# A new order of all steps, with other buffers and other engines for some, in an attention and FFN kernel on one core

## The chip, the core and the metric

The kernel runs on one core of a Trainium2 chip. A core has TensorE (PE: matmuls, and the weight loads PEld beside them), VectorE (DVE), ScalarE (ACT), GpSimd (POOL) and SyncE (SP), whose queue starts the DMAs here. The time is that of one execution in device microseconds: a median of 245.04 us over 3 runs (244.92 to 245.08).

## The reference

Polysketch attention, whose result goes into a multiplicative FFN:

```python
# q, k, v: 4 x 4 x 1088 x 32;  S1, S2: 8 x 32
def phi(x):
    a = np.einsum('rd,bhsd->bhsr', S1, x)
    b = np.einsum('rd,bhsd->bhsr', S2, x)
    return np.einsum('bhsi,bhsj->bhsij', a, b).reshape(*x.shape[:-1], r * r)
q_p, k_p = (phi(q), phi(k))
kv = np.einsum('bhsf,bhsd->bhfd', k_p, v)
z = np.sum(k_p, axis=2)
num = np.einsum('bhsf,bhfd->bhsd', q_p, kv)
den = np.einsum('bhsf,bhf->bhs', q_p, z)[..., None] + 1e-06
x = (num / den), reordered to 4352 x 128
# w1, w2: 128 x 1024;  w3: 1024 x 1024;  w_out: 1024 x 128
a = x @ w1
b = x @ w2
h = a * b @ w3
out = h @ w_out
```

## The kernel before

The program is a list of 1179 small named steps, each of which issues one instruction or a few. Nothing is decided at run time: the table ORDER names every step in the order in which it is issued, and each engine, SP's DMA queue included, runs its own instructions in just that order (every instruction is chained to the one before it on its engine). A step that waits therefore holds up all later steps of its engine.

Four more tables go with ORDER. SLOTS says for each kind of buffer which slot every allocation takes, in order: `b` are the eight PSUM banks, `m`, `l`, `s`, `x`, `raw` and `q_m` SBUF slots. A slot that is taken again makes its new writer wait for the last reader of what it held. POOL is the set of steps that run on GpSimd, where such a step has a choice; CPV that of the PSUM copies that run on VectorE instead of ScalarE. WARM gives the numbers of idle matmuls in the steps warm0 to warm11, 27 at the start and 2, 3, 4, 4, 4, 1, 2, 1, 1, 2, 2 later.

The steps have names by stage:

- `s.` prepares the sketches S1 and S2.
- `k0.` to `k3.` are the batches of keys and values (`kr.` their rest rows): loads, a maximum, a split of k in a leading and a rest part, `gram` (many short matmuls, L659), the small chain `G`, `T`, `N` (L883 to L912) which gives the numbers by which queries are centred, `kp` (the features of k), `kv` (L769), and `kzt`, `kqt`.
- `q0.` to `q6.` are groups of queries (`qr.` the rest rows): transposes, the sketch products `A0`, `A1`, `C0`, `C1`, the chain of splits `sm`, `st`, `sh`, `sl` (L1137 to L1157 on VectorE), products `p01`, `p2`, `p12`, the denominator `dn`, `de`, `rc`, the features `phi`, their transposes `pt`, and the attention product `x`, with `xs`, `xt`, `xc`, `xT` for q0, whose last, `xT` (L1291), is what the first FFN matmul reads.
- `g0.` to `g7.` and `gr.` are the FFN on groups of 512 rows (`gr` 256): for each of eight chunks of the width, `a` and `b` (matmuls with w1 and w2, L1799 and L1809), `c` (a copy of a out of PSUM), `m` (the product, L1815) and `o` (the matmul with the folded w3 and w_out, L1835, and L1824 for `gr`).
- `w` steps split the FFN's weights, `f` steps fold w3 and w_out in one matrix.
- `h4.` and `h6.` do the groups 4, 5 and 6, 7 in pairs by a scheme of seven products: matmuls `a1` to `b7` (L1673), sums `m11` to `m22` and `T1` to `T4` on VectorE and GpSimd (L1685 to L1742), products `P1` to `P7` (L1759; two for low and high partitions run side by side), and the sums `k1` to `k9` that give the two outputs (L1767 to L1785).
- `oT`, `oS`, `st` transpose, scale and store an output (L1842, L1848, L1556; `st1` of the rest rows L1562).

Bulk loads have one more rule: each waits until the fourth bulk load ahead of it has landed.

Of the kernel before, what the change touches and what calls it, by code (L numbers as in the profile page):

```python
# [65 lines left out]
    g0.0c g0.1c h4.1ac h4.1ad h6.1bc h6.2ad k0.kT1 k1.kvc k2.kT1 k2.kq k3.kT0 k3.kT1 k3.kq q0.xc0  # L66
    q0.xc1 q6.xT0 q6.xT2
# [15 lines left out]
q0.al k0.Nf q0.phi0 q0.phi1 q0.A1 q0.smy w1.m1 k1.max q0.sty q0.shy k0.kv3 k0.kv1 k0.kv2 q0.sly s.KS k0.kvr kr1.tr
k0.kvm w1.m0 kr1.kT q0.p01 q1.C0 q1.C1 q0.C1 k0.kzt k2.loadr q0.pt0 q0.C1t q0.scy q0.p2 k0.kz q0.pt1 k0.kvc kr1.ab
k0.kqt q0.p12 q0.dn q0.de q0.rc w1.j0 q0.pc0 q0.pc1 q0.x0 k1.kT0 q0.x1 q0.xs0 q0.xs1 q0.xt0 w1.a0 q1.A0 k2.load
w0.load k1.lead0 q0.xc0 q0.xc1 k0.kq w1.a1 k2.max q0.xt1 k1.ab q0.xT0 q0.xT1 g0.4a q1.load g0.5a q1.sm w0.m1 q1.st
q1.Ct g0.4c g0.4b q1.sh q1.sl k1.rest0 g0.7b w0.c1 g0.7a k1.abt w0.j1 k1.gram0 w0.c0 s.RC q1.scy k1.gram1 kh2.load
q1.sca q2.tr g0.5c q1.al q1.p01 q1.p2 k1.gram2 k1.gram3 kr1.abc k1.gram4 w6.load w0.m0 g0.6b w0.j0 g0.7c g0.7m k1.Gm
q1.p12 k1.Gc g0.0a w2.load w0.a1 q1.dn q1.de q1.rc q1.bs k1.Gt g0.3a k1.Ga k1.T0 k2.kT1 k1.Gb g0.3c q1.restT g0.2a
q1.phi k1.T1 q1.pt0 g0.4m w0.a0 q2.max q2.l2 g0.6a k1.Ta k2.lead0 k2.rest0 g0.1a g0.2c k1.Tc g0.5b q3.tr g0.5m k1.Tb  # L90
q1.pc0 q1.pt1 g0.1b w9.load k1.N0 s.AR q2.l1 q2.rm v3.zero q1.pc1 k1.N1 q1.x g0.6c g0.1c k1.Na k1.Nr k3.zero k2.gram0
g0.1m k2.gram1 k2.gram2 q3.max k2.gram3 g0.0c k2.kT0 k1.Nb q1.xT k2.gram4 q3.l2 k2.ab q2.A0 q2.C0 q2.C1 q3.l1 k1.kp0
v1.zero w9.c k2.abt g1.5a g1.5c g1.1a q2.Ct g1.7a q2.At q3.rm q3.A0 k0.Nr q2.sm q3.C0 q3.C1 k2.Gm v1.loadr q2.st w2.m
q2.sh g1.1c g1.2a k1.kp1 g0.6m q3.Ct g1.0a g1.7b k3.load v1.load g1.5b q3.At k2.Gt k3.loadr w2.c k2.Ga g0.0b w9.j
q2.sl g1.7c w6.c g1.6a k1.kv0 q3.sm k2.Gb w5.load q2.sc q2.al g1.0c k2.Gc g1.7m q2.p01 q3.st k1.kv2 k1.kv3 q3.sh w9.m
k1.kv1 k2.T0 k1.kvr q3.sl q2.p2 k2.T1 q2.p12 q2.dn q2.de g1.4a q2.rc k3.max g0.3b g0.0m g1.1b kh3.load g1.4c k2.Ta
g1.2b q3.sc g1.2c w5.c k2.Tc k1.kvc k1.kqt k1.kq g0.3m q3.p01 g1.6c g1.3a g1.5m g1.3b q2.bs q2.phi0 q2.pT0 g1.2m g1.3c
# [1837 lines left out]
```

## Time and profile before

| | |
|---|---|
| time, median of 3 runs | 245.04 us |
| span of the profiled execution | 244.1 us |
| PE busy | 236.2 us (97%) |
| DVE busy | 206.7 us (85%) |
| POOL busy | 161.9 us (66%) |
| ACT busy | 123.5 us (51%) |
| moved by DMA | 22.06 MB |

The profiled execution's span is 0.9 us below the median: the span runs from its first instruction to its last. In rows of the timeline the columns are start, length, engine, line of the kernel, operation, output and inputs, tile shape and how often; what stands in brackets is the engine's idle time ahead of the row, with what ended it. In rows of the chain of waits that ended last there are only start, length and what ran.

### The profile page before, as it was taken

Reading aid. Unit: us, or ns where it says so; the run is one execution under the profiler, and the core shown is the slowest. Engines: PE = TensorE matmul, PEld = TensorE weight load, DVE = VectorE, ACT = ScalarE, POOL = GpSimd, SP = SyncE. Lnnn points to the kernel's source line nnn. Section 1 sums busy time; section 2 is a strip of 40 time slices with the busy share of each in tenths; the row PEclk is TensorE's granted clock in tenths of the full one; section 3 lists DMA queues with packets and bytes.
Section 4 is the critical chain, followed back from the end, with each engine's and each line's share of the span. In section 5 each row is a group of like instructions: output and inputs, shape, how many; then the busy total and the mean of one; then the engine's idle time right before and its main releaser. Section 6 shows DMA issues by size and latency. Waiting matters only on the chain.

```text
span 244.1 us, 6745 instructions
## 1 busy us (share of the span) xinstructions
PE 236.2 (97%) x2724; PEld 129.8 (53%) x2724; DVE 206.7 (85%) x421; ACT 123.5 (51%) x246; POOL 161.9 (66%) x203
## 2 busy tenths in 40 slices
PE   8998999899999999999999999999999999999994
PEld 5887454545545646766566444444443354463363
DVE  2876988999899998997899878498989789999792
ACT  3976957675666764593012914355651164730010
POOL 4576658344856998764583889929999425883670
PEclk9999999999999999999999999999999999999999
DMA  7959797078859897200000000360000000000054
GB/s 201 265 143 325 181 227 190 6 197 224 220 141 251 188 217 190 59 1 3 3 0 0 4 0 3 59 113 3 1 0 0 0 3 0 0 1 3 12 90 93
DMA packets 31935, 22.06 MB, mean 90 GB/s; under 512 B 21280, under 2 KB 26528, under 8 KB 31904
## 3 DMA queue, kind: packets, MB, share of 16 engines
q1 hardware_dynamic: 31360, 21.11, 35.1%
q8 instruction: 21, 0.34, 0.6%
q10 hardware_dynamic: 544, 0.52, 0.6%
q14 instruction: 10, 0.08, 0.1%
HBM read 19.40 MB, written 2.23 MB: 89 GB/s over the span
## 4 chain that ended last, share of the span: by engine, by line
PE 87%; DMA 5%; ACT 2%; POOL 2%; DVE 1%; issue 1%; POOLq 0%; SPq 0%
PE b_ps L1809 12%; PE ps_o L1835 12%; PE ps_X L1673 11%; PE a_ps L1799 11%; PE ps_o L1759 10%; PE ps_w3o L534 6%; PE ps_Y L1673 6%; PE ps_Z L1673 3%; PE ps_g L659 2%; PE ps_x L1527 2%; PE ps_ac L1374 2%; DMA qh<-in_q_dram 2%; DMA k<-in_k_dram 2%; PE ps_or L1824 2%; POOL ph L1208 1%; PE idle_ps L255 1%
## 5 line engine op out<-in xcount | busy, mean ns | idle before, releaser
L1673 PE MATMUL ps_X<-xd,wv 64*128 64x512 f32 x112 | 36.3, 593 | 0.0
L1799 PE MATMUL a_ps<-xT,w 128*128 128x512 f32 (+1 forms) x80 | 36.1, 562 | 0.0
L1809 PE MATMUL b_ps<-xT,w 128*128 128x512 f32 (+1 forms) x80 | 35.6, 555 | 0.0
L1804 ACT COPY ffa<-a_ps 128x512 f32<-128x512 f32 (+1 forms) x38 | 20.1, 540 | 29.2 <-PE a_ps L1799 26.7
L1707 POOL TENSOR_TENSOR hc<-hc 128x512 f32<-128x512 f32 x16 | 20.7, 1304 | 15.7 <-DVE hc L1685 15.5
L1835 PE MATMUL ps_o<-ab,w3o 128*128 128x512 f32 x64 | 29.6, 600 | 0.0
L1680 ACT COPY hc<-ps_X 128x512 f32<-128x512 f32 x38 | 21.3, 590 | 16.1 <-PE ps_X L1673 12.9
L1815 DVE TENSOR_TENSOR ab<-ffa,b_ps 128x512 f32<-128x512 f32 (+1 forms) x40 | 23.9, 623 | 4.9 <-PE b_ps L1809 4.1
L501 POOL TENSOR_TENSOR w3c<-w3c,cv_m 128x512 int32<-128x512 int32 x16 | 21.2, 1344 | 4.2 <-DVE w3c L495 4.1
L1673 PEld LDWEIGHTS ps_X<-xd,wv 64*128 64x128 f32 x112 | 14.9, 186 | 13.1 <-issue 10.9
L1799 PEld LDWEIGHTS a_ps<-xT,w 128*128 128x128 f32 x80 | 14.1, 189 | 13.9 <-issue 8.8
L1809 PEld LDWEIGHTS b_ps<-xT,w 128*128 128x128 f32 x80 | 14.4, 190 | 13.1 <-issue 8.1
L1673 PE MATMUL ps_Y<-xd,wv 64*128 64x512 f32 x48 | 19.7, 594 | 0.0
L1835 PEld LDWEIGHTS ps_o<-ab,w3o 128*128 128x128 f32 x64 | 11.6, 190 | 13.4 <-issue 13.0
L534 PEld LDWEIGHTS ps_w3o<-wo,w3T 128*128 128x128 f32 x128 | 15.3, 192 | 2.4 <-issue 2.4
L534 PE MATMUL ps_w3o<-wo,w3T 128*128 128x128 f32 x128 | 15.7, 276 | 0.0
L1759 PE MATMUL ps_o<-hc,w3o 128*64 128x512 f32 x32 | 15.1, 595 | 0.0
L1759 PE MATMUL ps_o<-tt,ws 128*64 128x512 f32 x32 | 13.7, 594 | 0.0
L1680 ACT COPY hc<-ps_Y 128x512 f32<-128x512 f32 x14 | 8.1, 592 | 9.7 <-PE ps_Y L1673 6.6
L263 ACT ACTIVATE cv_c<-raw 128x1024 f32<-128x1024 f32 (+1 forms) x13 | 13.0, 1014 | 0.0
L1540 ACT COPY xd<-ps_x 64x256 f32<-64x256 f32 x24 | 8.8, 367 | 7.2 <-PE ps_o L1835 6.8
L1497 POOL COPY nz<-nz 32x8 f32<-32x8 f32 x32 | 11.1, 347 | 1.4
(347 smaller groups left out, 593.0 us busy)
## 6 DMA issues: line engine op xcount, KB each, us to landing
raw<-in_moe_w_dram SPq DMA_DIRECT2D x32, 256.0 KB, 5.0
qh<-in_q_dram SPq DMA_DIRECT2D x4, 544.0 KB, 4.5
raw<-in_moe_w_dram SPq DMA_DIRECT2D x4, 512.0 KB, 5.8
out_dram<-oT SPq DMA_DIRECT2D x32, 64.0 KB, 2.0
k<-in_k_dram SPq DMA_DIRECT2D x3, 512.0 KB, 5.1
v<-in_v_dram SPq DMA_DIRECT2D x2, 512.0 KB, 6.1
kh<-in_k_dram SPq DMA_DIRECT2D x8, 128.0 KB, 3.6
raw<-in_moe_w_out_dram SPq DMA_DIRECT2D x4, 256.0 KB, 5.0
```

The lines of the kernel that those rows point to most:

```text
L263: act.activation(dst, hi.bitcast(F32), ACT.Prelu, scale=2.0 ** -112, alpha=-2.0 ** 32)
L501: pool.tensor_tensor(d, d, x["m"][:, i * 512:(i + 1) * 512], ALU.add)
L534: pe.matmul(t["o"], w3T[ko][:, c], wo[:, c], start=c == 0, stop=c == NC - 1)
L1673: pe.matmul(x[bank], stat(j, u)[:, i * 128:(i + 1) * 128], rows(j, u), start=new, stop=True, tile_position=(u * 64, 0), skip_group_check=True)
L1680: cp(n(y))(x[k], x[bank])
L1707: on(f"h{g}.{i}m{k}").tensor_mul(both[0][k], both[0][k], both[1][k])
L1759: pe.matmul(acc_o[bank][half[0]:half[1]], w(i), x(i), start=n == 1, stop=n == (2 if j == 3 else 4), tile_position=(0, half[0]), skip_group ...
L1799: pe.matmul(x["a"][:, :w], w_of(0, c), xT[g][:, c0:c0 + w], start=True, stop=True)
L1804: cp(f"g{g}.{c}{su}c")(x["s"][:, :w], x["a"][:, :w])
L1809: pe.matmul(x["b"][:, :w], w_of(1, c), xT[g][:, c0:c0 + w], start=True, stop=True)
L1815: dve.tensor_mul(ab_sb[g, c][:, c0:c0 + w], x["s"][:, :w], x["b"][:, :w])
L1835: pe.matmul(o_ps[g], w3o[:, c], ab_sb[g, c], start=n == 1, stop=n == NC)
```

## The change

ORDER differs from the 61st step on; the first 60 steps are the same. All steps issue what they issued. SLOTS has other numbers for the kinds b, l, m, q_m, raw, s and x. POOL is a set of 101 steps: 28 steps go from GpSimd to VectorE and 39 the other way. CPV changes so that 17 copies go from ScalarE to VectorE and 10 back. WARM stays, but warm7 to warm11 stand elsewhere. All line numbers behind POOL are one higher, since the table has a line more.

```diff
 SLOTS = {
     "b": 
-        "012345670214657210671306537457462512346127340273014526045721472352140327540542370673245716"
...
+        "012345670214567201573105367142357165237604325160671250432761406401326475013472650407265120"
...
-    "q_m": "0110110",
-    "raw": "010212120211221",
+    "q_m": "0101010",
+    "raw": "012012021202102",
...
 CPV = set("""
-    g0.0c g0.1c h4.1ac h4.1ad h6.1bc h6.2ad k0.kT1 k1.kvc k2.kT1 k2.kq k3.kT0 k3.kT1 k3.kq q0.xc0
-    q0.xc1 q6.xT0 q6.xT2
+    g0.1c g0.5c g1.2c g2.5c h4.0bd h4.1bc h4.1be h4.3bc h4.3be h6.0ae h6.1ac h6.1be k0.kT0 k0.kT1
+    k1.kvc kr1.kT q1.pc0 q4.xT1 q4.xT3 q6.xT0 q6.xT1
 """.split())
...
-k1.zero s.Pm warm5 q0.l1 q0.A0 warm6 kr0.ab k0.lead1 q0.rm q0.sma q0.sta warm7 k0.kT0 v0.load v0.loadr k1.load k0.ab1
+k1.zero s.Pm warm5 q0.l1 q0.A0 warm6 kr0.ab k0.lead1 q0.rm q0.sma v0.load k0.ab1 k0.kT0 q0.sta kr1.load w0.load warm11
...
```

Three places at which it shows. The first is VectorE ahead of the first FFN matmul: L1198 is q0.rc, L1274 q0.xc, L1291 q0.xT, and L1137 to L1157 are q1's split. Before:

```order
L1194 SCALAR_TENSOR_TENSOR s_rc<-s_d 128x16
L1198 RECIPROCAL s_rc<-s_rc 128x16
L466 TENSOR_SCALAR w_81<-cv_c 128x2x256
L1274 COPY xc<-ps_xt 128x256 x2
L1291 TENSOR_TENSOR xT<-xc,ps_xs 128x256 x2
L1137 TENSOR_REDUCE s_g<-ps_a 128x32
```

Now (one line higher each):

```order
L1199 RECIPROCAL s_rc<-s_rc 128x16
L1138 TENSOR_REDUCE s_g<-ps_a 128x32
L202 SCALAR_TENSOR_TENSOR s_t_654<-s_g,ps_a 128x256
L205 SCALAR_TENSOR_TENSOR s_hl<-s_g,s_t_654 128x2x128
L1131 STREAM_TRANSPOSE ay_C<-ps_c 128x384
L1158 TENSOR_TENSOR s_hl<-ps_a,s_hl 128x2x128
L1292 TENSOR_TENSOR xT<-xc,ps_xs 128x256 x2
```

The five steps of q1's split stand ahead of xT now, the copies xc are gone to ScalarE, and the conversion of w1 stands further ahead.

The second is TensorE where k2's gram begins (L659, alternating rows of two kinds). L912 is k1.N, L1297 q1.x. Before:

```order
L1809 MATMUL b_ps<-xT,w_81 128x512
L912 MATMUL ps_N<-T_p,P2a 32x8 x4
L912 MATMUL ps_N<-T_p,P2b 32x8 x4
L912 MATMUL ps_N<-T_p,P2s 32x8 x8
L1297 MATMUL ps_x<-pT,kz_605 64x512 x2
L659 MATMUL ps_g<-kk 32x64
L659 MATMUL ps_g<-k,kk 32x32
```

Now (L884 is the first of k1.T):

```order
L1810 MATMUL b_ps<-xT,w_81 128x512
L1800 MATMUL a_ps<-xT,w_81 128x512 x2
L1810 MATMUL b_ps<-xT,w_81 128x512 x2
L1800 MATMUL a_ps<-xT,w_81 128x512
L884 MATMUL ps_T<-RS,G_a 32x32
L660 MATMUL ps_g<-kk 32x64
L660 MATMUL ps_g<-k,kk 32x32
```

The gram stands behind six FFN steps and a part of T; k1.N and q1.x come behind it.

The third is TensorE's end: L1759 are the products P of the groups 6 and 7, L1799, L1809 and L1824 the rest rows' a, b and o. Before:

```order
L1824 MATMUL ps_or<-w3o,ab 128x128 x3
L1759 MATMUL ps_o<-hc,ws 64x512 x2
L1824 MATMUL ps_or<-w3o,ab 128x128
L1799 MATMUL a_ps<-xT,w_81 128x256
L1809 MATMUL b_ps<-xT,w_81 128x256
L1759 MATMUL ps_o<-hc,ws 64x512 x2
L1799 MATMUL a_ps<-xT,w_81 128x256
L1824 MATMUL ps_or<-w3o,ab 128x128
L1809 MATMUL b_ps<-xT,w_81 128x256 x3
```

Now:

```order
L1760 MATMUL ps_o<-hc,ws 64x512
L1800 MATMUL a_ps<-xT,w_81 128x256
L1810 MATMUL b_ps<-xT,w_81 128x256 x2
L1800 MATMUL a_ps<-xT,w_81 128x256
L1825 MATMUL ps_or<-w3o,ab 128x128
L1810 MATMUL b_ps<-xT,w_81 128x256 x2
L1825 MATMUL ps_or<-w3o,ab 128x128 x3
L1810 MATMUL b_ps<-xT,w_81 128x256
L1825 MATMUL ps_or<-w3o,ab 128x128 x12
```

All products P stand ahead of what is left of the rest rows; before, the last four stood among it.

More of the change, by code (lines that the diff above doesn't have):

```diff
@@ L83 @@
[L83 to L97, printed above, removed]
```

144 lines of the change are left out of this document (80 added, 64 removed).

## The prediction

> **What bounds the kernel now.** I read the page first, then the windows, the stalls of TensorE in the timeline, and last the end of the program on all engines. The page:
>
> ```profile
> span 244.1 us, 6745 instructions
> ...
> PE 236.2 (97%) x2724; PEld 129.8 (53%) x2724; DVE 206.7 (85%) x421; ACT 123.5 (51%) x246; POOL 161.9 (66%) x203
> ```
>
> TensorE (PE) is busy for 236.2 of 244.1 us, so a new order of the same instructions can gain only in the remaining 7.9 us, or by making the matmuls themselves cheaper. The windows say where the 7.9 us are (columns: start and end, length, then busy time and count of PE, weight loads, DVE, ACT, POOL, then the granted clock, which is 1.00 nearly everywhere, and DMA):
>
> ```profile
> 0.00:10.00 10.00, 8.72 (x93) 6.73 (x93) 4.82 (x16) 5.33 (x16) 3.64 (x34) 1.00 0.79 214
> 10.00:20.00 10.00, 9.03 (x261) 7.81 (x253) 7.55 (x26) 8.47 (x18) 7.80 (x15) 1.00 0.73 225
> 20.00:30.00 10.00, 9.31 (x167) 6.28 (x167) 8.15 (x23) 7.90 (x18) 6.05 (x9) 1.00 0.80 229
> 30.00:40.00 10.00, 9.76 (x172) 5.03 (x171) 8.54 (x24) 7.07 (x18) 6.78 (x7) 1.00 0.90 215
> 40.00:50.00 10.00, 8.84 (x280) 5.24 (x279) 8.91 (x23) 5.42 (x10) 5.47 (x7) 1.00 0.23 59
> 27.40:49.10 21.70, 20.30 (x456) 11.01 (x454) 19.14 (x46) 15.07 (x30) 13.62 (x18) 1.00 0.63 152
> 49.10:240.50 191.40, 191.40 (x1769) 99.24 (x1764) 169.32 (x317) 89.27 (x171) 133.08 (x135) 1.00 0.28 65
> ```
>
> From 49.10 to 240.50 PE has no gap at all. Before that it is idle for 1.28 + 0.97 + 0.69 + 0.24 + 1.16 = 4.34 us, the first 1.0 of which is the start; 3.6 us lie behind 240.5. The kernel thus has three parts: a beginning in which PE waits now and then (what can be gained there is under 3.3 us), a middle that is PE work, and a tail. Who ends the idle times of the beginning:
>
> ```profile
> 14.27 0.22 PE L659 MATMUL ps_g<-k,kk 128*32 128x32 f32 x1 [0.41 <-issue]
> ...
> 20.35 0.69 PE L769 MATMUL ps_kv<-kp,v 128*32 128x64 f32 x34 [0.91 <-issue]
> ...
> 26.01 0.44 PE L1287 MATMUL ps_xs<-ident,xs 128*128 128x128 f32 x2 [0.34 <-ACT xs L1280]
> ...
> 38.37 0.66 PE L1246 MATMUL ps_ph<-ident,ph 128*128 128x128 f32 x4 [0.24 <-POOL ph L1208]
> ...
> 46.98 0.19 PE L659 MATMUL ps_g<-k,kk 128*32 128x32 f32 x1 [1.16 <-issue]
> ```
>
> Three are marked "issue": PE waited for nothing that the profile shows, 2.48 us in sum. All three fall inside a run of very short matmuls (grams and kv), and the page has a queue that carries nothing but instructions:
>
> ```profile
> q8 instruction: 21, 0.34, 0.6%
> ```
>
> 0.34 MB in 21 packets is 16 KB each. 2724 matmuls and 2724 weight loads by 21 packets are about 260 instructions a packet. I read the three stalls as PE running out of program: some 260 short instructions pass faster than the next 16 KB arrive. [...]
>
> **The change, term by term.** The first 60 steps are the same. The terms are set against the profiled execution (span 244.1 us, about 0.9 under the median of 245.04; I move the median by the same sum).
>
> *Term 1, the first FFN matmul.* DVE on the way to it, and PE's first FFN pass:
>
> ```profile
> 20.98 0.52 DVE L204 SCALAR_TENSOR_TENSOR s_hiy<-s_gy,s_t 128x128 f32<-128x128 f32 x1
> ...
> 23.20 0.32 DVE L1068 STREAM_TRANSPOSE ay_C<-ps_cy 128x128 f32<-128x128 f32 x1 [1.38 <-PE ps_cy L1030]
> ...
> 25.27 0.25 DVE L1198 RECIPROCAL s_rc<-s_rc 128x16 f32<-128x16 f32 x1
> 25.44 0.36 DVE L466 TENSOR_SCALAR w<-cv_c 128x512 int32<-128x512 int32 x1
> 25.71 0.74 DVE L1274 COPY xc<-ps_xt 128x256 f32<-128x256 f32 x2
> 26.48 0.79 DVE L1291 TENSOR_TENSOR xT<-xc,ps_xs 128x256 f32<-128x256 f32 x2
> 27.19 0.42 DVE L1137 TENSOR_REDUCE s_g<-ps_a 128x32 f32<-128x256 f32 x1
> ...
> 29.26 1.35 DVE L651 TENSOR_TENSOR kk<-k,kk 128x1152 f32<-128x1152 f32 x1
> ...
> 32.95 0.38 DVE L1176 TENSOR_TENSOR s_pr<-s_hl 128x256 f32<-128x256 f32 x1
> ...
> 27.42 1.96 PE L1799 MATMUL a_ps<-xT,w 128*128 128x512 f32 x4
> ```
>
> The change does q0's C products ahead of the kv products on PE. In the rows before, DVE waits 1.38 us for them and the 0.91 us stall stands ahead of them; I take the transpose at 23.20 to come 2.0 us earlier, at 21.2. But three steps of 1.3 us in sum now stand behind it (s_hiy 0.52, q0's p01, which on DVE takes the 0.38 of q1's at 32.95, and one more half of w1, 0.36 as at 25.44), and the five q1 steps (27.19 to 29.26, 2.07 us) stand ahead of xT. The two copies to xc, 0.74 us, go to ACT. From the transpose to the end of xT were 27.27 - 23.20 = 4.07 us; now 4.07 + 1.26 + 2.07 - 0.74 = 6.66. So xT ends at about 27.9, and the first FFN pass, 0.15 behind it as before, starts at about 28.1, with 0.1 for the one extra handover to ACT 28.2: **+0.75**. Ends: 27.2 if the transpose comes 1 us earlier still, 28.9 if PE delivers nothing earlier than 21.9.
>
> *Term 2, stalls behind it.* In 27.40:49.10 PE is idle for 1.40 us, of which 1.16 is the stall at 46 and 0.24 the wait for POOL's ph. The stall at 46 stands in k2's gram, which comes right behind k1's N products and q1.x, so that hundreds of short instructions follow one another. In the change that gram stands behind six FFN steps of two passes each (5.2 us) and N comes later, so the next lines have time to arrive: **-1.40**. Ends: nothing (it only moves) and -1.40.
>
> *Term 3, warm matmuls.*
>
> ```profile
> 6.46 0.38 PE L255 MATMUL idle_ps<-zeros 128*128 128x256 bf16 x2
> ...
> 7.11 0.49 PE L255 MATMUL idle_ps<-zeros 128*128 128x256 bf16 x3
> ```
>
> One more costs 0.11. Four of them (warm7 twice, warm8, warm9) stood in gaps ahead of the first FFN pass and now stand among work that does not wait: **+0.44**.
>
> *Term 4, changes of tile shape on PE.*
>
> ```profile
> 64.55 0.86 PE b_ps L1809 x2
> ...
> 66.73 1.05 PE b_ps L1809 x2
> ```
>
> Two passes that follow passes of the same shape cost 0.86 (0.43 each); the first two behind a block of narrow matmuls cost 1.05. Going out costs about as much, so a change of shape is 0.1 us. In program order the change has 63 where there were 75: eight fewer ahead of 49 us, half of which I place behind the first FFN pass, and four fewer in the tail, counted there. **-0.4**, ends 0 and -0.8. [...]
>
> *Term 5, new waits in the middle.* PE has no wait there before, so nothing is to be won and something may be lost. The nearest rows, from the stretch from the end of q6's attention products to the first seven-product matmul:
>
> ```profile
> 110.00:155.00 45.00, 45.00 (x476) 24.66 (x475) 36.76 (x76) 15.54 (x39) 32.01 (x29) 1.00 0.01 2
> ...
> L1707 POOL TENSOR_TENSOR hc<-hc 128x512 f32<-128x512 f32 x16 | 20.7, 1304 | 15.7 <-DVE hc L1685 15.5
> ...
> 181.62 8.77 POOL L1497 COPY nz<-nz 32x8 f32<-32x8 f32 x16
> ...
> 231.65 3.56 POOL L1497 COPY nz<-nz 32x8 f32<-32x8 f32 x16
> ```
>
> The steps that the change puts on POOL in this stretch take 13 us more by each one's own duration, 32 + 13 of 45: full, yet PE needs the result at its end only. I put one short new wait or moved instruction fetch somewhere in the middle: **+0.3**, ends 0 and 2. The last two rows are a warning: the same sixteen POOL copies take 8.77 us in one place and 3.56 in another. [...]
>
> *Term 6, the tail.* PE's products of the second half of the seven-product scheme, the output chain on DVE and POOL, and the stores on SP's queue:
>
> ```profile
> 220.48 10.45 PE ps_o L1759 x48
> ...
> 238.16 2.39 PE L1824 MATMUL ps_or<-w3o,ab 128*128 128x128 f32 x20
> 230.18 0.68 DVE L1779 TENSOR_TENSOR oc<-oc,ps_o 64x512 f32<-64x512 f32 x1 [1.08 <-PE ps_o L1759]
> ...
> 236.65 0.71 DVE L1842 STREAM_TRANSPOSE oT<-oc 128x512 f32<-128x512 f32 x1
> 237.50 1.05 POOL L1848 TENSOR_TENSOR oT<-oT,nz 128x512 f32<-128x512 f32 x1 [1.13 <-DVE oT L1842]
> 236.40 4.19 SPq L1556 DMA_DIRECT2D out_dram<-oT  x8
> ...
> 240.95 0.62 SPq L1562 DMA_DIRECT2D out_dram<-oT  x1
> ```
>
> Before, the chain k3 (230.18), k2, ... ends with g7's transpose at 237.36; its eight stores with g6's end at 240.59, and the last store, of the rest rows, waits for PE (240.55) and starts at 240.95. Both paths end together. Now all 28 products, 28 x 0.435 (10.45 for the 24 of the row, two passes each) = 12.2 us, stand in one block, and the last one that k3 needs stands 2.6 us before its end (three side-by-side pairs of two passes, 0.86 each, follow it). From that: k3 at X - 2.4 (X is the block's end), seven k steps and a transpose by 0.72, then k9, one more FFN product on DVE, and g7's transpose ends at X + 5.4; POOL's product 1.05, four stores by 0.5 (4.19 for 8) behind it, and the last store starts at X + 9.0. The block starts 0.43 later in the remaining work than before, as one more rest pass stands ahead of it. So the last store comes 0.43 + 12.2 + 9.0 = 21.6 us behind where the block used to start (220.48), against 240.95 - 220.48 = 20.5: **+1.1**. PE itself ends 7 to 8 us behind X (seven passes of 0.43, sixteen of 0.24, and DVE's products that they wait for), so it is the stores that end last. Ends: 0 (the order of waits is kinder than I think) and +1.5.
>
> Sum: 0.75 - 1.40 + 0.44 - 0.4 + 0.3 + 1.1 = +0.8, and 245.04 + 0.8 = 245.8.
>
> **The rivals.**
>
> *Faster: xT is not late.* If the five q1 steps on DVE fill time in which xT waits for the xs and xt products anyway (PE's row at 26.01 shows such a wait, 0.34), 2.07 us of term 1 are no cost: the first FFN pass starts at 26.1, term 1 is -1.3, and the time 245.8 - 2.05 = 243.8; half of it, 244.8. For it: xs and xc still run on ACT. Against it: xT needs DVE itself, which is in order.
>
> *Slower: the fetch stalls only move.* The same instructions need the same 21 packets, and the 1.16 us come back at another run of short matmuls, such as q3.x with k2.kv, on top of term 5: 245.8 + 1.16 = 247.0. [...]
>
> *Slower: POOL ahead of h4.* Six sums of weights (1.3 us each by the nearest row, L1707's mean of a POOL sum of 512 columns) now stand among q4's and q6's last steps in POOL's queue. If its 45 us are overrun by one of them, PE waits 1.3 us at the first seven-product matmul, 247.1; it decides where POOL's steps run over 10% longer than their rows. [...]
>
> *The order does nothing.* PE's work is the same, and the gain of the beginning is what the tail gives back, or the tail stays hidden behind PE: 245.8 - 1.1 + 0.3 = 245.0.
>
> **How the numbers follow.** Forecast 0.42, its own range 245.0 to 246.6; faster rival 0.30 (243.7 to 244.9); fetch 0.12; POOL 0.07; nothing 0.09. 0.2% is 0.49 us, about what a measurement of this kernel can tell. Faster than 244.55: 0.24 of the faster rival and 0.03 of the last, 0.27. Slower than 245.53: 0.32 of the forecast and the two slower rivals, 0.51. The rest, 0.22, is the same. The range from 243.8 to 247.0 leaves out about 0.05 below and 0.12 above.
>
> **What would show it.** PE's first FFN row at 28.2 (term 1; 26.1 for the faster rival). No "issue" row near 46 (term 2); an "issue" row of a microsecond elsewhere is the fetch rival. PE 10.00 of 10 in every window from 50 to 230 (term 5); a gap at about 155 with POOL as releaser is the POOL rival. In the tail the last store over 1.5 us behind PE's last matmul (term 6; before 0.4). I am wrong if a gain of the beginning is kept to the end, or if DVE has a new stall in the middle that I have not seen.

## The result: 5% slower, and the profile after

The change makes the kernel slower: 259.87 us (median of 4 runs, 256.74 to 262.16) against 244.98 us of the kernel before on the same chip, a ratio of 1.0535 with a 95% interval of 1.0483 to 1.0587. The kernel was run once more later: 258.60 us, 1.0527 (1.0484 to 1.0571). Medians here are over all executions of a kernel, while ratios compare only those within 1.5% of the kernel's fastest, and none is given where there is just one such execution. The profiled execution is the one of 256.74 us, the fastest of its four; its span is 254.8 us, 10.7 us more than that of before. The accounts below are made on that pair, so they explain 10.7 us of a loss that is 14.9 us by the medians. What makes the other executions longer isn't the clock: the four have mean granted clocks of 0.984 to 0.987 and spans of 254.8 to 260.2 us, and the longest ones have the higher clock.

The page of the changed kernel, the busy times and the chain of waits that ended last:

```profile
span 254.8 us, 6759 instructions
...
PE 241.4 (95%) x2724; PEld 136.6 (54%) x2724; DVE 222.8 (87%) x423; ACT 116.3 (46%) x233; POOL 177.3 (70%) x214
...
PE 75%; DVE 14%; DMA 4%; issue 3%; POOL 2%; SPq 1%; POOLq 0%; DVEq 0%
```

And the chain of the kernel before, from its page:

```profile
PE 87%; DMA 5%; ACT 2%; POOL 2%; DVE 1%; issue 1%; POOLq 0%; SPq 0%
```

VectorE was hardly on the way to the end before (1%); now it is 14% of it. Busy time on DVE is up by 16.1 us and on POOL by 15.4, while ACT lost 7.2 (17 copies went from ScalarE to VectorE and 13 came back, not 10): one and the same work got dearer by being placed otherwise.

The windows of the changed kernel (columns as before: length, then PE, PEld, DVE, ACT, POOL, the granted clock, DMA):

```profile
0.00:10.00 10.00, 8.67 (x93) 6.69 (x93) 4.87 (x16) 5.35 (x16) 3.65 (x34) 1.00 0.80 216
10.00:20.00 10.00, 7.79 (x218) 7.07 (x207) 5.80 (x18) 5.52 (x12) 5.92 (x11) 0.83 0.90 273
20.00:30.00 10.00, 8.59 (x207) 6.55 (x206) 8.90 (x32) 9.54 (x24) 4.50 (x7) 1.00 0.82 221
30.00:40.00 10.00, 9.12 (x181) 4.59 (x162) 8.94 (x14) 8.06 (x15) 6.18 (x5) 1.00 1.01 218
40.00:50.00 10.00, 7.99 (x174) 4.63 (x175) 8.54 (x24) 4.61 (x8) 8.78 (x11) 0.83 0.75 200
50.00:100.00 50.00, 48.95 (x781) 25.66 (x779) 48.34 (x101) 29.40 (x53) 41.89 (x36) 1.00 0.67 168
```

Up to 50 us PE is now idle for 1.33 + 2.21 + 1.41 + 0.88 + 2.01 = 7.84 us, 3.50 more than before; from 50 to 100 it is idle for 1.05, where it had no gap. And the granted clock, 1.00 everywhere before, is 0.83 in two windows of 10 us: 2 x 0.17 x 10, about 3.4 us of matmul time lost. Finer windows show what such a 0.83 is made of:

```profile
14.00:16.00 2.00, 1.77 (x9) 1.71 (x9) 0.76 (x3) 0.00 (x0) 0.00 (x0) 0.61 1.03 318
16.00:18.00 2.00, 2.00 (x62) 1.87 (x65) 0.40 (x1) 1.71 (x3) 1.42 (x1) 0.54 0.95 240
42.00:44.00 2.00, 1.99 (x3) 0.95 (x4) 2.00 (x4) 2.00 (x3) 2.00 (x4) 0.50 0.80 236
44.00:46.00 2.00, 2.00 (x41) 0.74 (x43) 0.99 (x5) 1.14 (x3) 1.43 (x3) 0.71 0.58 142
```

The clock falls to half, stays there for about 3.4 us and comes back: up to 1.7 us are lost each time. Both phases begin at a place where TensorE had just waited. Its waits in the timeline:

```profile
14.23 0.30 PE L820 MATMUL ps_krt<-ident,kr 128*128 128x128 f32 x1 [1.83 <-DMA kr<-in_k_dram]
...
21.82 0.24 PE L913 MATMUL ps_N<-T_p,P2a 32*32 32x8 f32 x8 [0.88 <-DVE T_p L205]
24.07 0.42 PE L1031 MATMUL ps_cy<-q,RS 128*32 128x128 f32 x8 [0.49 <-POOL RS L950]
30.93 1.98 PE L1800 MATMUL a_ps<-xT,w 128*128 128x512 f32 x4 [0.32 <-DVE xT L1292]
...
42.01 1.22 PE L1810 MATMUL b_ps<-xT,w 128*128 128x512 f32 x1 [2.57 <-POOL w L471]
```

The first wait is for a load. SP's queue shows why it is late; k1's rest rows stand right behind v0's 512 KB now:

```profile
5.32 0.43 SPq L583 DMA_DIRECT2D v<-in_v_dram  x1
5.80 1.84 SPq L610 DMA_DIRECT2D kr<-in_k_dram  x2
```

In the chain of waits that load is one piece of its own:

```profile
6.58 7.51 DMA kr<-in_k_dram
```

The last wait is for GpSimd. Its rows ahead of 42 us, and under them VectorE's row in the same time:

```profile
36.33 4.25 POOL L215 TENSOR_SCALAR kk<-k,k_g 128x1152 f32<-128x1152 f32 x1 [1.26 <-ACT q L1344]
...
40.70 1.26 POOL L471 TENSOR_TENSOR w<-w,cv_m 128x512 int32<-128x512 int32 x1
```

```profile
36.58 3.68 DVE L1195 SCALAR_TENSOR_TENSOR s_rc<-s_d 128x16 f32<-128x16 f32 x1
```

L215 is `k2.lead0`, one of the steps that the change puts on GpSimd. It takes 4.25 us there. On VectorE, before the change, its kind took 0.85:

```profile
L214 DVE TENSOR_SCALAR kk<-k,k_g x3: 546/848/861, 8.1 to 64.8; 128x1152 f32<-128x1152 f32 x2, 128x512 f32<-128x512 f32 x1
```

(durations of one in ns: lowest, median, highest). And VectorE loses time beside it: L1195 on 128x16 took 0.18 and 0.27 us in the two places where it ran before; here it lasted 3.68, to 40.26, while GpSimd's step ended at 40.58. Compared with the fastest instance of the same operation and shapes in the traces before and after, 17 VectorE instructions are stretched by more than 0.12 us before the change, 9.4 us in sum; 42 of them, 29.2 us, after it, every one beside a running GpSimd instruction. These 19.8 us more exceed the whole growth of VectorE's busy time, 16.1.

The account of the 10.7 us: idle time of PE +3.50 up to 50 us, +1.05 up to 100, +0.15 behind it; half clock +3.3 (PE stood idle for 0.25 us of the second phase); the last store starts 1.2 us behind PE's last matmul, before 0.4: +0.8. PE ends at 250.41 instead of 240.55, 9.86 later; what the idle time and the clock leave of that, about 1.9 us, is longer matmul time, and which matmuls it comes from stayed open.

### The profile page after: what moved, and what is told of

It reads as the page before. It is cut to its first block, busy times and chain, and to the rows that moved or that the text cites. A ratio compares the mean times of both kernels' runs of the same rounds, so it can differ in the third digit from the quotient of the medians.

```text
span 254.8 us, 6759 instructions
## 1 busy us (share of the span) xinstructions
PE 241.4 (95%) x2724; PEld 136.6 (54%) x2724; DVE 222.8 (87%) x423; ACT 116.3 (46%) x233; POOL 177.3 (70%) x214
## 4 chain that ended last, share of the span: by engine, by line
PE 75%; DVE 14%; DMA 4%; issue 3%; POOL 2%; SPq 1%; POOLq 0%; DVEq 0%
PE ps_X L1674 11%; PE ps_o L1836 11%; PE ps_o L1760 9%; PE a_ps L1800 8%; PE b_ps L1810 8%; PE ps_w3o L535 6%; PE ps_Y L1674 5%; PE ps_Z L1674 3%; DMA kr<-in_k_dram 3%; PE ps_g L660 3%; DVE ab L1816 2%; PE ps_x L1528 2%; DMA qh<-in_q_dram 1%; DVE q L1353 1%; PE ps_ac L1375 1%
## 5 line engine op out<-in xcount | busy, mean ns | idle before, releaser
L1810 PE MATMUL b_ps<-xT,w 128*128 128x512 f32 (+1 forms) x80 | 37.9, 576 | 3.0 <-POOL w L471 2.6
L1674 PE MATMUL ps_X<-xd,wv 64*128 64x512 f32 x112 | 40.4, 598 | 0.0
L1800 PE MATMUL a_ps<-xT,w 128*128 128x512 f32 (+1 forms) x80 | 37.6, 573 | 0.8 <-DVE RC L938 0.4
L1805 ACT COPY ffa<-a_ps 128x512 f32<-128x512 f32 (+1 forms) x36 | 18.7, 544 | 31.5 <-PE a_ps L1800 25.8
L1816 DVE TENSOR_TENSOR ab<-ffa,b_ps 128x512 f32<-128x512 f32 (+1 forms) x40 | 24.0, 617 | 4.2 <-PE b_ps L1810 3.7
L1681 ACT COPY hc<-ps_X 128x512 f32<-128x512 f32 x33 | 18.7, 589 | 16.4 <-PE ps_X L1674 14.9
L1674 PEld LDWEIGHTS ps_X<-xd,wv 64*128 64x128 f32 x112 | 17.2, 186 | 9.9 <-issue 5.9
L1674 PE MATMUL ps_Y<-xd,wv 64*128 64x512 f32 x48 | 20.6, 595 | 0.0
L1760 PE MATMUL ps_o<-hc,ws 128*64 128x512 f32 x32 | 14.9, 597 | 0.0
L539 ACT COPY w3o<-ps_w3o 128x128 f32<-128x128 f32 x8 | 2.1, 266 | 22.9 <-PE ps_w3o L535 22.9
L1686 DVE TENSOR_TENSOR hc<-hc,ps_Z 128x512 f32<-128x512 f32 x16 | 10.6, 678 | 2.0 <-ACT hc L1681 1.0
```

Of the source, the lines that this page charges most:

```text
L1674: pe.matmul(x[bank], stat(j, u)[:, i * 128:(i + 1) * 128], rows(j, u), start=new, stop=True, tile_position=(u * 64, 0), skip_group_check=True)
L1681: cp(n(y))(x[k], x[bank])
L1760: pe.matmul(acc_o[bank][half[0]:half[1]], w(i), x(i), start=n == 1, stop=n == (2 if j == 3 else 4), tile_position=(0, half[0]), skip_group ...
L1800: pe.matmul(x["a"][:, :w], w_of(0, c), xT[g][:, c0:c0 + w], start=True, stop=True)
L1805: cp(f"g{g}.{c}{su}c")(x["s"][:, :w], x["a"][:, :w])
L1810: pe.matmul(x["b"][:, :w], w_of(1, c), xT[g][:, c0:c0 + w], start=True, stop=True)
```

## The experiments

Four theories for the loss, beside each other: **L**, the two lead steps on GpSimd; **K**, the load of k1's rest rows behind v0; **E** and **O**, that the loss belongs to the sets of engines or to the order, each by itself; and **C**, the half clock. Later ones have their letter in the expectation that brings them in: S and V, VectorE steps that GpSimd steps beside them make late; Q, the order of the loads; W, a wait. D, VectorE being short of time itself, stands against V in the last kernel: waits and median as in the one that it starts from, 255 to 256. Each kernel is the changed one with one edit, unless said otherwise.

### The lead steps back on VectorE

```diff
-    h6.3T4 h6.s3 h6.s4 k0.Nf k0.kp0 k1.Nr k1.kp0 k1.kp1 k2.Nr k2.kp0 k2.kp1 k2.lead0 k3.kp1 k3.lead0
+    h6.3T4 h6.s3 h6.s4 k0.Nf k0.kp0 k1.Nr k1.kp0 k1.kp1 k2.Nr k2.kp0 k2.kp1 k3.kp1
```

> The change with two of its 39 steps taken back from GpSimd to VectorE: k2.lead0 and k3.lead0. Theory L (these two are what is dear: 4.25 us each on GpSimd against 0.86 on VectorE before, and one VectorE instruction beside each of them stretches to 3.68 and 3.08 us; w0.a0 behind the first comes late and TensorE waits 2.57 us with its clock at 0.50 afterwards): 4 to 5 us less than the change, that is 252 to 253 against the 256.7 of the profiled run, no gap of TensorE at 40 us, and q1.de and q3.rm back under 0.8 us. Theory K (kr1's late load is what costs): under 1.5 us less, the gap at 12.4 us stays. Theory S (many GpSimd steps slow VectorE everywhere): under 1.5 us less, sum of VectorE's times as in the change.

Measured: 257.22 us. One of the four executions, with a mean granted clock of 0.998, took 251.79 us; the other three, at 0.980 to 0.986, took 256.69 to 258.33. The wait of 2.57 us at 42 is gone, but the clock falls to half later instead, behind a wait for VectorE at 90 us:

```profile
90.00:100.00 10.00, 9.74 (x166) 6.59 (x165) 9.84 (x16) 5.87 (x13) 5.65 (x5) 0.83 0.22 54
```

The gap was L's, as expected. The gain is 1.4 to 2.7 us by the medians (against the two measurements of the changed kernel), less than the 4 to 5 that L had, and four executions that lie 6.5 us apart don't settle it.

### The load of k1's rest rows first

```diff
-k1.zero s.Pm warm5 q0.l1 q0.A0 warm6 kr0.ab k0.lead1 q0.rm q0.sma v0.load k0.ab1 k0.kT0 q0.sta kr1.load w0.load warm11
+k1.zero s.Pm warm5 q0.l1 q0.A0 warm6 kr0.ab k0.lead1 q0.rm q0.sma kr1.load v0.load k0.ab1 k0.kT0 q0.sta w0.load warm11
```

> The change with kr1.load issued ahead of v0.load instead of behind it. Theory K (TensorE waits 1.83 us at kr1.tr for a load that lies behind v0's 512 KB, its clock falls to 0.54 to 0.61 for some 3 us, and the first FFN pass comes at 30.9 in place of the predicted 28.2): no wait at kr1.tr, clock 1.00 from 10 to 20 us, first FFN pass near 28.2, and 2.5 to 3.5 us less than the change. Theory L: first FFN pass earlier, but the gap at 40 us takes it back, under 1 us less.

Measured: 257.88 us, ratio 1.0416 (1.0325 to 1.0507). That is 2.0 us less than the change by the medians, and the intervals overlap (1.0483 to 1.0587 there). The kr wait is gone, the clock stays at 1.00 there, and the first FFN pass comes 1.63 us earlier:

```profile
10.00:20.00 10.00, 7.16 (x221) 6.45 (x212) 7.43 (x21) 7.40 (x17) 7.98 (x13) 1.00 0.88 272
...
16.14 0.19 PE L660 MATMUL ps_g<-k,kk 128*32 128x32 f32 x1 [1.04 <-issue]
18.30 0.22 PE L884 MATMUL ps_T<-RS,G_a 128*32 128x32 f32 x2 [0.96 <-DVE G_a L205]
19.60 0.65 PE L686 MATMUL ps_kt<-ident,k 128*128 128x128 f32 x4 [0.85 <-DMA k<-in_k_dram]
...
29.30 1.98 PE L1800 MATMUL a_ps<-xT,w 128*128 128x512 f32 x4 [0.33 <-DVE xT L1292]
```

K held for its own wait. But three others of a microsecond each appear behind it: PE is idle for 2.84 us of these ten, more than the 2.21 before the edit. At 40 us PE then waits 2.75 for L471, since that place did not move; no half clock follows it there (1.00 from 40 to 50).

### Both

The two edits together.

> Both edits. If K and L are separate and together the cause of most of the 10.7 us: 249 to 250.5 (7 us less than the change's 256.7), with the rest from VectorE's longer times and the tail. Theory S: 254 or more.

Measured: 253.45 us, 1.0308 (1.0260 to 1.0355): 5 to 6 us come back, the largest step of all: less than L and K together were to give (249 to 250.5), and a little more than S allowed (254 or more). What stands next is the loads; the chain of waits runs over them nearly without a break from 7 to 37 us, and ends in a wait of 2.47 us at 37.79 for ScalarE's q:

```profile
7.10 7.02 DMA v<-in_v_dram
14.18 5.88 DMA kh<-in_k_dram
20.14 6.23 DMA k<-in_k_dram
26.39 3.26 DMA raw<-in_moe_w_dram
29.66 7.12 DMA raw<-in_moe_w_dram
```

### The lead steps alone, in the kernel before

The other direction: the kernel before, with only `k2.lead0` and `k3.lead0` put on GpSimd.

```diff
-    k1.kp1 k2.kp0 k2.kp1 k2.rest0 k3.kp0 k3.kp1 q0.al q0.p01 q0.phi1 q0.sca q1.al q1.bs q1.p12
+    k1.kp1 k2.kp0 k2.kp1 k2.rest0 k2.lead0 k3.lead0 k3.kp0 k3.kp1 q0.al q0.p01 q0.phi1 q0.sca q1.al q1.bs q1.p12
```

> The kernel before with k2.lead0 and k3.lead0 moved to GpSimd, nothing else. Theory L: each takes about 4.2 us there and stretches a VectorE instruction beside it to 3 us or more; k2.rest0 and kp behind it on GpSimd come 4 us later; 1.5 to 4 us slower than before. Theory S: within 0.5 us of before, since only two of the 39 steps move.

Measured: 249.36 us, 1.0159 (1.0112 to 1.0207): two steps of 1179 cost 4 us, at the upper end of L's range; S, within 0.5 us of before, falls here. The three parts of it stand in the trace: the wait, the half clock behind it, and a wait of 1.7 us for VectorE (L1815) later.

```profile
45.71 0.34 PE L659 MATMUL ps_g<-kk 128*32 128x64 f32 x8 [2.38 <-POOL kk L651]
```

```profile
44.00:46.00 2.00, 0.29 (x22) 0.29 (x26) 1.97 (x3) 1.97 (x3) 2.00 (x4) 1.00 0.00 0
46.00:48.00 2.00, 2.00 (x137) 2.00 (x127) 1.97 (x6) 0.40 (x1) 0.11 (x1) 0.64 0.00 0
48.00:50.00 2.00, 2.00 (x72) 1.15 (x63) 1.41 (x3) 0.00 (x0) 1.54 (x3) 0.51 0.08 15
```

The half clock is not bound to the new order: here the gap of 2.38 us was made in the old one, and 3.4 us at 0.50 follow 0.9 us behind it.

### Engines or order, one without the other

Three kernels with the tables mixed: the new ORDER and SLOTS with the old POOL and CPV; the old ORDER and SLOTS with the new POOL and CPV; and the first of them with kr1's load ahead of v0's. The first of the edits, cut (POOL's other lines and CPV are exchanged in the same way):

```diff
-    g4.oS g5.oS g6.oS g7.oS h4.0T1 h4.0T2 h4.0T3 h4.0T4 h4.0m11 h4.0m22 h4.1T1 h4.1T3 h4.1m11
+    g4.oS g5.oS g6.oS g7.oS h4.0T1 h4.0T2 h4.0T3 h4.0m12 h4.0m22 h4.1T2 h4.1m11 h4.1m12 h4.2m11
...
```

> The change's order and buffers with the engine sets of before (POOL and CPV as before, so k2.lead0 and k3.lead0 are back on VectorE too). Theory E (the engine sets are the larger part: b1 lost 4 us by two steps alone): 247 to 250, with the wait at kr1.tr left. Theory O (the order is the larger part): 252 or more, and VectorE still over 9.5 of 10 busy from 50 to 100 us.

> The order and buffers of before with the engine sets of the change. Theory E: 250 to 254, that is at least 1 us more than b1's 249.4, which has two of these moves. Theory O: as b1, 249 to 250, since the other 37 steps cost nothing where the order has room for them.

> The change's order with kr1.load first and the engine sets of before. If kr1, the two lead steps and the other engine moves are all there is: within 1.5 us of before, 244 to 247. If the order itself has a further cost: 249 or more, and the profile shows which waits are left.

Measured: 275.58 us (270.83 to 278.22); 298.96 us, ratio 1.2148 (1.2090 to 1.2206); and 272.43 us, ratio 1.0938 (1.0874 to 1.1001). Both mixtures are far slower than either kernel, so E and O both fall as separate causes: an order fits only the engines for which it was laid out. The largest waits of TensorE in the second, from the list of waits (engine, line, releaser: us in sum, times, longest):

```profile
PE ps_ph L1247 <- DVE pT L1253: 5.0, 1, 5.0
PE ps_o L1760 <- POOL tt L1743: 5.0, 2, 4.2
PE a_ps L1800 <- DVE ab L1816: 3.4, 1, 3.4
```

A step that changes its engine is late for its new neighbours, and every later step of that engine with it.

### The clock by idle matmuls

The smallest edit against the first half clock: sixteen more idle matmuls ahead of the kr wait.

```diff
-WARM = [27, 2, 3, 4, 4, 4, 1, 2, 1, 1, 2, 2]
+WARM = [27, 2, 3, 4, 4, 4, 1, 2, 1, 1, 18, 2]
```

> The change with 16 more idle matmuls (1.8 us by 0.11 each) ahead of kr1.tr, in the gap in which TensorE waits for kr1. Theory C (half of what that wait costs is the clock, which stands at 0.50 for 3.4 us behind it, 1.7 us lost each time): no clock below 0.95 between 10 and 20 us, the load lands no earlier, and 1.0 to 1.7 us less than the change (median near 258.3). Theory W (only the waiting costs): within 0.5 us of the change, 259.4 to 260.4.

Measured: 260.68 us, 1.0591 (1.0531 to 1.0650). Neither theory's range holds it. The clock holds from 10 to 20, and the first FFN pass comes 1.04 us earlier than in the change, at 29.89, much as C has it. But nothing is left of that at the end: half clock stands in two later windows, and a wait of 1.97 us, marked issue, is new at 51.89. One execution shows how much of the loss is not the clock's: its mean granted clock was 0.999, and its span still 256.7 us, 11 us or more above the kernel before in the same measurement (242.8 to 245.4), of which the added idle matmuls can be at most 1.8.

```profile
10.00:20.00 10.00, 8.56 (x225) 7.65 (x225) 6.88 (x16) 6.75 (x16) 6.68 (x13) 1.00 0.91 271
40.00:50.00 10.00, 8.96 (x177) 5.03 (x178) 8.29 (x24) 5.57 (x9) 8.55 (x11) 0.83 0.82 217
90.00:100.00 10.00, 8.25 (x153) 4.86 (x152) 9.81 (x13) 4.71 (x11) 5.05 (x7) 0.83 0.62 156
```

### The loads

From here on both first edits (lead steps, kr1) are in. First w0's load goes behind k1's, so that k1's keys don't queue behind half a megabyte of weights (`w0.load` is taken out of the line shown above):

```diff
-k0.gram2 k0.gram3 q0.C0t q1.l2 k0.gram4 k0.Gm k0.Gt k0.Ga q1.l1 k0.Gc k0.Gb k1.load k0.kp0 q0.sca w0.m0 k0.kv0 kr0.abc
+k0.gram2 k0.gram3 q0.C0t q1.l2 k0.gram4 k0.Gm k0.Gt k0.Ga q1.l1 k0.Gc k0.Gb k1.load w0.load k0.kp0 q0.sca w0.m0 k0.kv0 kr0.abc
```

> a3 (kr1.load first, the two lead steps on VectorE) with w0.load issued behind k1.load instead of ahead of it. Theory Q (the order of the loads: the change issues w0's 512 KB and v0 ahead of k1 and kr1, and the chain of waits of a3 runs from 7 to 37 us over loads alone): no wait of TensorE at k1's transposes (1.38 us in a3), first FFN pass 0.5 to 1.5 us earlier than a3's 29.4, and 1 to 2.5 us less than a3 (253.5). Theory V (by then VectorE sets the time): first FFN pass earlier, the end as a3 within 0.7 us.

Then, on top of it, q1's load ahead of w9's:

```diff
-q0.p12 q0.dn q1.C0 w9.load q1.C1 w1.j0 w1.a0 q0.de k0.kz q0.rc w0.c0 q1.sm k0.kvc q0.x1 q0.x0 s.KS k1.kT0 q0.xs0 q1.st
+q0.p12 q0.dn q1.C0 q1.load w9.load q1.C1 w1.j0 w1.a0 q0.de k0.kz q0.rc w0.c0 q1.sm k0.kvc q0.x1 q0.x0 s.KS k1.kT0 q0.xs0 q1.st
```

> a7 with q1.load (544 KB, issued at 26.3 us in the change and at 21.3 before) ahead of w9.load. Theory Q: the wait of TensorE near 37 us that goes back to ScalarE's work on q2 (2.5 us in a3) goes, and with it the clock's 1.7 us behind it: 249 to 251. Theory V: as a7 within 0.7 us.

And the other direction in the kernel before, w0's load early:

```diff
-k1.zero s.Pm warm5 q0.l1 q0.A0 warm6 kr0.ab k0.lead1 q0.rm q0.sma q0.sta warm7 k0.kT0 v0.load v0.loadr k1.load k0.ab1
+k1.zero s.Pm warm5 q0.l1 q0.A0 warm6 kr0.ab k0.lead1 q0.rm q0.sma q0.sta warm7 k0.kT0 v0.load w0.load v0.loadr k1.load k0.ab1
...
-w0.load k1.lead0 q0.xc0 q0.xc1 k0.kq w1.a1 k2.max q0.xt1 k1.ab q0.xT0 q0.xT1 g0.4a q1.load g0.5a q1.sm w0.m1 q1.st
+k1.lead0 q0.xc0 q0.xc1 k0.kq w1.a1 k2.max q0.xt1 k1.ab q0.xT0 q0.xT1 g0.4a q1.load g0.5a q1.sm w0.m1 q1.st
```

> The kernel before with w0.load ahead of k1.load, as the change has it, and nothing else. Theory Q: k1, kr1 and k2 land about 2 us later, TensorE waits for k1's transposes or kr1.tr, and the time is 1.5 to 4 us over before. Theory V: within 0.5 us of before.

Measured: 255.48 us, 1.0353 (1.0287 to 1.0420); 256.00 us, 1.0385 (1.0336 to 1.0435); 248.31 us, 1.0097 (1.0078 to 1.0116). The early load costs about 2.4 us in the kernel before. That is in Q's range, but only 0.65 us of it is the wait of k1's transposes that Q named. More of it stands in waits marked issue: the two shown in the prediction at 14.27 and 20.35 grow from 0.41 and 0.91 us to

```profile
15.99 0.22 PE L659 MATMUL ps_g<-k,kk 128*32 128x32 f32 x1 [1.59 <-issue]
...
23.07 0.69 PE L769 MATMUL ps_kv<-kp,v 128*32 128x64 f32 x34 [1.16 <-issue]
```

In the changed order the same move brings nothing that can be told from the kernel with both edits (the intervals 1.0287 to 1.0420 and 1.0260 to 1.0355 overlap). Its profiled execution, 252.61 us, has the least idle time of all of these; the wait of 1.38 us at k1's transposes is gone, as Q had it, and so is that of 2.47 us for ScalarE's q, so that q1's load ahead of w9's had nothing left to win there. But it has waits for VectorE of 0.94 and 0.87 us, and 6.83 us of half clock behind them:

```profile
18.04 0.22 PE L884 MATMUL ps_T<-RS,G_a 128*32 128x32 f32 x2 [0.94 <-DVE G_a L205]
19.95 0.29 PE L913 MATMUL ps_N<-T_p,P2a 32*32 32x8 f32 x8 [0.87 <-DVE T_p L205]
```

```profile
20.00:30.00 10.00, 10.00 (x195) 8.28 (x195) 8.04 (x29) 9.03 (x22) 4.71 (x7) 0.66 0.93 247
```

### The changed kernel once more

The changed kernel, without an edit, to see what of its account comes back in another execution.

> The change itself once more, beside the others on the same chip: 257 to 262, with the clock at 0.50 for 3.4 us in two or three places that need not be those of the first profile (14 and 42 us).

Measured: 258.60 us. The waits for kr (1.6 us) and for L471 (2.56) and both windows of 0.83 are there again; a wait of 1.6 us for VectorE's L1816 is new in the profiled execution, which the first one had not.

### What is left: clock or VectorE

Two kernels on top of the one with both first edits and w0 later. The first takes warm7 to warm9 back to where PE thins out, ahead of k0's T and N products and k1's transposes, with 6 to 8 idle matmuls each (the banks in SLOTS follow the new order):

```diff
-WARM = [27, 2, 3, 4, 4, 4, 1, 2, 1, 1, 2, 2]
+WARM = [27, 2, 3, 4, 4, 4, 1, 6, 8, 8, 2, 2]
...
-k0.kv3 k1.loadr kh3.load q0.al w1.c1 q1.rm q0.phi0 k0.T0 k0.Ta k0.T1 k1.tr1 k0.Tb k2.zero k0.Tc k0.N0 k0.Na w0.m1
+k0.kv3 k1.loadr kh3.load q0.al w1.c1 q1.rm q0.phi0 warm8 k0.T0 k0.Ta k0.T1 k1.tr1 k0.Tb k2.zero k0.Tc warm9 k0.N0 k0.Na w0.m1
...
```

> The a7 order with the warm matmuls put where PE thins out: 8 ahead of the first T product, 8 ahead of the first N product and 6 ahead of k1's transposes of the second half, in place of one or two much later. They add about 19 x 0.11 = 2.1 us of idle matmuls, most of it into waits of 0.5 to 0.95 us that PE has there anyway. Theory C (the half clock behind the short waits is what is left of the loss): no phase of clock 0.50 at 19 to 26 us in the profiled run, 1.7 to 3.4 us less, a median of about 252.5. Theory V (VectorE steps beside GpSimd steps are late, and PE waits for them whatever its clock): the clock holds there, but the median stays within 1 us of 255.5, or the drop comes elsewhere.

The second puts `k0.kp0` and `q0.phi0` back on VectorE, and the halves `k0.kp1` and `q0.phi1` on GpSimd, as they were:

```diff
-    h6.3T4 h6.s3 h6.s4 k0.Nf k0.kp0 k1.Nr k1.kp0 k1.kp1 k2.Nr k2.kp0 k2.kp1 k3.kp1
-    q0.al q0.phi0 q0.sca q1.p01 q1.p12 q1.phi q1.sca q2.al q2.p01 q2.p12 q2.phi0 q2.sc q2.sl q3.bs
+    h6.3T4 h6.s3 h6.s4 k0.Nf k0.kp1 k1.Nr k1.kp0 k1.kp1 k2.Nr k2.kp0 k2.kp1 k3.kp1
+    q0.al q0.phi1 q0.sca q1.p01 q1.p12 q1.phi q1.sca q2.al q2.p01 q2.p12 q2.phi0 q2.sc q2.sl q3.bs
```

> The a7 kernel with four steps changed in engine: k0.kp0 and q0.phi0 back on VectorE, k0.kp1 and q0.phi1 on GpSimd, as before the change. In a7 q0.sha (0.25 us by its fastest) took 2.04 us beside k0.kp0 on GpSimd, k0.Ta 0.63 instead of 0.17 beside q0.phi0, and PE waited 0.94 and 0.87 us for the T chain right behind. Theory V: sha takes 0.25 again, the two waits shrink under 0.5 us, the half clock behind them goes, median 252 to 253.5. [...]

Measured, the first: 253.59 us, 1.0302 (1.0218 to 1.0387). The phase of half clock at 20 is gone, and with it perhaps 2 us (the intervals overlap); the profiled execution has another one at 91. Three of its four executions had a mean granted clock of 0.997 to 1.000 and spans of 250.0 to 252.5 us, while the three executions of the kernel before at 1.000 took 242.6 to 243.9. So 6 to 10 us are left that have next to nothing to do with the clock, of which up to 2 can be the added idle matmuls; C alone falls.

The second: 257.79 us, 1.0478 (1.0403 to 1.0554), not better (the interval just overlaps that of the kernel that it starts from). The expectation that `q0.sha` would run in 0.25 us was wrong. VectorE, and below it GpSimd:

```profile
13.24 2.05 DVE L205 SCALAR_TENSOR_TENSOR s_hla<-s_ga,s_t 128x128 f32<-128x128 f32 x1
15.32 0.29 DVE L1098 TENSOR_TENSOR s_hla<-ps_a,s_hla 128x128 f32<-128x128 f32 x1
```

```profile
12.89 2.25 POOL L678 TENSOR_TENSOR kp<-kab 128x1024 f32<-128x1024 f32 x1 [1.84 <-ACT kab L709]
```

The other half, `k0.kp1`, now runs on GpSimd at the same time, and `q0.sha`, which has two inputs in SBUF, ends 0.15 us behind it, whichever half it is. The next one, L1098, reads one of its inputs from PSUM and takes 0.29. So the hold on VectorE follows the GpSimd instruction here, from one half to the other; what its absence would bring is not shown, as this kernel did not get rid of it. On top comes a wait of TensorE of 2.30 us. The list marks it issue, but VectorE's rows say what it is:

```profile
17.30 1.31 DVE L678 TENSOR_TENSOR kp<-kab 128x1024 f32<-128x1024 f32 x1
```

```profile
18.72 0.65 PE L770 MATMUL ps_kv<-kp,v 128*32 128x64 f32 x32 [2.30 <-issue]
```

The `kv` product reads `kp`, and the half that the edit put on VectorE ends at 18.61, 0.11 us ahead of it. So TensorE waits for the moved step itself, behind the held one, which speaks for theory D: VectorE has no time to spare there.

What remains of the loss, in the list of TensorE's waits, the start left out, summed by the engine that ended them (us, profiled executions):

| kernel | VectorE | GpSimd | ScalarE | loads | issue |
|---|---|---|---|---|---|
| before | 0 | 0.2 | 0.3 | 0.3 | 2.5 |
| changed | 2.5 | 3.1 | 0 | 2.1 | 0 |
| changed, once more | 4.7 | 3.1 | 0 | 1.6 | 0 |
| lead steps back | 4.6 | 0.5 | 0 | 1.4 | 0 |
| both first edits | 2.3 | 0.5 | 2.5 | 1.9 | 0.5 |
| and w0 later | 3.7 | 0 | 0 | 0 | 0.5 |
| and idle matmuls | 4.9 | 0 | 0.2 | 0 | 0.7 |
| before, lead steps on GpSimd | 1.7 | 2.6 | 0.3 | 0 | 0.2 |

The edits take away the waits for GpSimd and for loads. Waits for VectorE, of which the kernel before has none, are in every kernel of the table with the changed order, 2.3 to 4.9 us. No version beats the kernel before.

## Why the prediction was wrong, point by point

**The first FFN matmul (term 1, +0.75, at 28.2).** It came at 30.93. The walk along VectorE's rows was sound as far as it went: from the transpose to the end of xT it took 6.09 us, where 6.66 were forecast. What failed is its start, the transpose that was to come 2.0 us earlier, at 21.2:

```profile
24.78 0.32 DVE L1069 STREAM_TRANSPOSE ay_C<-ps_cy 128x128 f32<-128x128 f32 x1 [0.40 <-PE ps_cy L1031]
```

The term walked no loads: the line with `v0.load` and `kr1.load` stood in the diff, and behind 512 KB kr1's small load took 7.51 us to land. With kr1 first the transpose comes at 23.15 and the pass at 29.30; so 1.63 of the 2.73 us that were missed are this load and the half clock behind it. Even then the transpose is no earlier than before (23.20), since TensorE has new waits ahead of it (1.04, 0.96, 0.85 and 0.48 us) that were not priced either. The rival "xT is not late" falls with it.

**The stalls behind it (term 2, -1.40).** No issue row stands near 46, as forecast. But where PE was to be without a gap, it waits 2.57 us for GpSimd at 42, and loses 1.7 us more at half clock. This is the step that failed most: it counted what leaves and did not ask what is late next on the engine that the change fills. `k2.lead0` and `k3.lead0` were in the new set; neither is named in any term. They cost 4.25 us each instead of 0.85, and moved alone they cost 4 us of the kernel's time.

**Idle matmuls and tile shapes (terms 3 and 4, +0.44 and -0.4).** Neither was measured by itself. The price of a change of shape stands in the trace of before: passes of 512 columns start 0.43 us after one another, but the last ahead of narrow matmuls takes 0.52 and the first behind them 0.53. PE's time beside idle and clock went up by about 1.9 us, not by 0.04; the sum of the two is refuted, and which part is wrong was not tried.

**New waits in the middle (term 5, +0.3, from 0 to 2).** From 50 to 240 us PE is idle for 1.1 us, inside its ends. That is luck: in the later profile of the same kernel it is idle for 3.44 us from 50 to 100 alone, past them. The reason given was another: no gap stands ahead of the first product of the pairs of groups, and GpSimd releases none there; VectorE does. What was wrong is the price, "13 us more by each one's own duration", and that it was set for 110 to 155 us alone. A step that goes to GpSimd was paid twice here, by its own duration there, up to five times as long (4.25 us against 0.85), and by the VectorE instructions beside it: 17 stretched ones and 9.4 us became 42 and 29.2. The prediction has no term for that over the whole span; its rival of 0.07 looks at one spot, and at GpSimd's own time there.

**The tail (term 6, +1.1).** The block P of groups 6 and 7 starts at 230.83 and the last store at 251.64, 20.81 us apart; before 20.47. So +0.34, where the term had 12.2 + 9.0 = 21.2 for this stretch, +0.7: the direction was right, the size twice too large. The 0.43 for a rest pass ahead of the block isn't in this measure. The last store starts 1.2 us behind PE's last matmul; "over 1.5" was forecast.

**The rival of fetch stalls** did not happen in the changed kernel, in which PE has no issue row. That the stalls are PE running out of program is still a reading. What the trace of before has for it: the three waits marked issue, at 14.27, 20.35 and 46.98, ended 1.33, 1.41 and 1.55 us behind the landing of a packet of the instruction queue. But the stalls are no fixed price of a number of instructions, as I took them: 0.91 us became 1.16, and 0.41 became 1.59, when only a load was moved.

**The clock** has no term at all. It was 1.00 in every window of before, and I took that for a property of the kernel. But the same kernel with a gap of 2.38 us in it fell to 0.50, and in the change half clock is 3.3 of the 10.7 us.

What stays open: the 6 to 10 us that the best of the repaired kernels still lacks at nearly full clock are put down to waits for VectorE and longer matmul time by the table and the account above; no single edit has shown them, and the edit that should have taken the hold away at one place moved it instead.

## What to carry to other kernels

A new order must be read on all queues, SP's first: follow each load that stands behind a larger one, and price each step that changes its engine by a row of that engine, plus what the other engine loses beside it. With TensorE 97% busy, a gap can cost more than its length: behind that of 2.38 us stood 3.4 us at half clock, 1.7 us more. And do not mix an order with another's engines: the two mixtures were 16 and 39 us slower here than the slower of the two kernels.

## What the runs showed of the hardware

- The granted clock of TensorE fell to 0.50 for 3.41 or 6.83 us at a time. The windows of 1 us of all sixteen traces, from 0 to 95 and from 150 to 245 us, show 25 whole phases of 0.50 within TensorE's work, 16 of the first length and 9 of the second. In the changed kernel the clock stood at 1.00 for 23.89 us between its two phases, seven times 3.41.
- By the same windows TensorE was idle for about 1.4 to 3.4 of the 3.41 us ahead of each of the 27 falls that they show within its work. The least is 1.44 us, the wait of the first edit's kernel for kr, with the fall 1.6 us behind it. The two waits of 0.94 and 0.87 us with w0 later stood within 2.9 us, and 6.83 us at 0.50 followed. But no fall followed the wait of 2.75 us in the kernel with kr1 first, so the length of a wait alone does not decide it; what does was not shown.
- A VectorE instruction that works on SBUF alone was often stretched by a GpSimd instruction beside which it started. Counted are, over the traces before and after, the VectorE instructions that start beside a GpSimd instruction which outlasts their fastest instance: of operations on two tensors 32 of 37 were stretched by more than 0.12 us, and of TENSOR_SCALAR 4 of 4; of reductions, transposes and reciprocals none of 40 was. Of 210 instructions that read PSUM none was; with the lead steps alone on GpSimd, L1815 took its 0.69 us in the middle of the 4.26 us of such a step. In most rows a stretched one ends 0.15 us behind the GpSimd instruction with 128 columns and 0.55 with 512, as if it began only when the other ended: 2.05 us for one of 128x128. The longest, 3.68 us for one of 128x16, ended 0.33 ahead of it.
- A TENSOR_SCALAR of 128x1152 took 4.25 us on GpSimd and 0.85 on VectorE; a TENSOR_TENSOR of the same 128x1152 (L651, before the change) took 2.63 and 1.35, so that a move of the first cost five times its time, and one of the second twice.
